# The second product of the last 30 token blocks, made of seven half products instead of eight

## The chip, the cores and the metric

The kernel runs on one core of one Trainium2 chip. The metric is the device time of one execution in microseconds (us), the median of several runs. The core's engines work side by side and wait for each other through semaphores: PE (TensorE, matmuls; its weight loads are shown as PEld), DVE (VectorE), ACT (ScalarE), POOL (GpSimd) and SP (SyncE, which here issues DMAs). ACT and POOL issue DMAs as well.

## The reference, cut to what matters

Two parts follow each other. The first filters a batch of 8 sequences of 2496 positions and 256 channels in the frequency domain; the second sends each of the 19968 positions (tokens) through one of 8 experts, chosen by a hash of its token id:

```
Y = np.fft.rfft(x, axis=1) * (filt_r + 1j * filt_i)
y = np.fft.irfft(Y, n=2496, axis=1)                 # then (8*2496, 256)
expert_idx = token_ids * np.int64(2654435761) % 8
for e in range(8):
    xe = y[expert_idx == e]
    h = np.maximum(xe @ w1[e], 0.0)                  # 256 -> 1024
    out[expert_idx == e] = h @ w2[e]                 # 1024 -> 256
```

All data is float32.

## The kernel before, in words

**The filter.** Each of the 8 batches (class Batch) goes through stages of matmuls with tables: stage1 (L225) to a DRAM buffer, forward (L269) with a product by the filter on DVE (L275 to L280), back (L292) to a second DRAM buffer, stage3 (L225 again). scatter (L382) writes the rows, by an indirect DMA of POOL, into a DRAM array xs that is sorted by expert into blocks of 256 tokens. Table d_t serves forward, e_t serves back, f_t holds the filters.

**The experts.** There are 80 sure blocks (NSURE) and 5 that are run only if there are tokens left. step(i) (L864) does one block. up(i) (L795) makes h = relu(x w1): both matrices are cut in halves, and the product is made by a scheme of Winograd's kind from 7 half products instead of 8, from sums of tokens (token_sums, L783, on DVE) and sums of weights (weight_sums, L792, on POOL, 4 per block). Its half products go to PSUM banks a, b and c; ACT copies one out (L813), DVE adds (L809) and ACT takes the relu (L806). down(i) (L832) makes h w2 in the plain way, 16 matmuls of 256 columns into bank d (L837), and DVE copies the result out (L842). store(i) (L844) writes the rows of a block, two indirect DMAs of POOL (L847). A float32 matmul stands in the trace as two passes.

**Loads.** load(i + 2) (L753, ACT queue, L762) brings the tokens of a block, token_parts (L773) transposes them on DVE. weights(i + 2, 0) and (i + 2, 1) (L395) issue on SP the loads of w1 (L413) and w2 (L416), 1 MB each, under a condition: only where the expert of the block is another than that of the block two earlier. Even and odd blocks have buffers of their own.

**The order.** It is written out by hand. In step(i) the queues get: on POOL weight_sums(i + 1), then store(i - 1); on PE up(i), then down(i); on DVE the sums of up(i), then token_parts(i + 1) and token_sums(i + 1), then the copy of down(i). The filter's pieces hang in a list of due times counted in blocks (todo), and run_until puts those that are due between the parts of a block: run_until(i + .6) after up, three more among the matmuls of down, one at the block's end. The filter's last pieces are due at block 47, so from block 48 on a block holds nothing else. The last stage of blocks, 50 to 79, holds the tokens of the last two batches and what was left of the others; its blocks go through the experts in ascending order, even blocks through one half of them and odd ones through the other.

The order of up's half products, with what reads each, is short enough to show:

```
product("a", w1[:, 0, 0:h], x[0, 0], True)
nc.scalar.copy(out=h21, in_=ps["a"][:])
product("b", t[1], st[:, 1, :], True)
plus(h12, "b", h21)
product("c", t[0], st[:, 0, :], True)
plus(h22, "c", h21)
```

Of the kernel before, what the change touches and what calls it, by code (L numbers as in the profile page):

```python
# [11 lines left out]
F32 = mybir.dt.float32  # L12
I32 = mybir.dt.int32
AF = mybir.ActivationFunctionType
OP = mybir.AluOpType
# [4 lines left out]
P = 128  # L20
# [26 lines left out]
DP = C // P  # L47
# [3 lines left out]
NPAD = NT * TB - N  # L51
NQP = NPAD // P
NSURE = NT - 5

# [64 lines left out]
def kernel(  # L119
# [16 lines left out]

    xs = nc.dram_tensor("xs", (NT * TB, W), F32)
    slot_dram = nc.dram_tensor("slots", (N,), I32)

    def pool(stack, name, bufs, space=None):  # L140
        kw = {} if space is None else {"space": space}
# [32 lines left out]
    def slot(kind):  # L174
        slots[kind].append(slots[kind].pop(0))
        return slots[kind][-1]

    put_off = []

# [215 lines left out]
    def weights(i, which):  # L395

        if i >= NT:
            return
        if i >= 2 and which == 0:
            ws[i] = ws[i - 2][0:2]  # L400
        eng, kw = nc.scalar if i < 2 else nc.sync, {}
        if which == 0:
            ws[i].append(eng.value_load(chunk_i[0:1, 0, i:i + 1], min_val=0, max_val=E - 1))
            if i >= 2:
                ws[i].append(eng.value_load(chunk_i[0:1, 1, i:i + 1], min_val=0, max_val=1))
        e = ws[i][2]
        if i >= 2:
            kw = {"cond": ws[i][3]}
        if which == 0:


            for f in (slice(0, F // 2), slice(F // 2, F)) if i < 2 else (slice(0, F),):
                eng.dma_start(out=ws[i][0][:, :, f],  # L413
                              in_=moe_w1[bass.ds(e, 1)].rearrange("one (p dp) f -> p (one dp) f", p=P)[:, :, f], **kw)
        else:
            eng.dma_start(out=ws[i][1], in_=moe_w2[bass.ds(e, 1)].rearrange("one (fp p) d -> p (one fp) d", p=P), **kw)  # L416


    rctx = ctx.enter_context(ExitStack())
# [357 lines left out]
    def token_sums(i):  # L777
        x = parts[i]
        st = work.tile([P, 4, P], F32, name=f"st_{i}", tag="st")
        for k, (p, q, op) in enumerate((((1, 0), (1, 1), OP.add), (0, (0, 0), OP.subtract),  # L780
                                        ((0, 0), (1, 0), OP.subtract), ((0, 1), 1, OP.subtract))):
# [62 lines left out]
    def store(i):  # L844
        o = rows.pop(i)
        for h in range(2):
# [13 lines left out]
    def run_until(t):  # L860
        while main and main[0][0] < t:
            main.pop(0)[1]()

    def step(i):  # L864
        ht = work.tile([P, 2, FP, P], F32, name=f"ht_{i}", tag="ht")
# [12 lines left out]
        run_until(i + 1)  # L878
# [56 lines left out]
```

## Time and profile before

| | |
|---|---|
| median of 3 runs | 1490.96 us (1489.63 to 1495.55) |
| the profiled execution | 1492.68 us, its span 1490.90 us |
| mean granted TensorE clock | 0.977 |
| block 50 begins, block 79 ends (PE) | 1083.2, 1478.0 us |
| matmuls of the second product, L837 | 589.5 us busy, 2560 passes, mean 384 ns |
| weight sums on POOL, L792 | 316 of 774 us of POOL, mean about 1.3 us each |
| DMA | 245.70 MB, 165 GB/s in the mean |

The span is the time from the first to the last recorded instruction; the execution's time has 1.8 us around it. A row of the timeline gives the start (us from the span's start), the time taken, the engine, the line, the operation with what it writes and reads, the shape, how many of them the row merges, and in brackets how long the engine had been idle before and what ended that. Ends of matmuls are modelled, so the pace of PE is read from start to start. A line in the chain or the groups is that of the kernel's file as printed above.

### The profile page before, as it was taken

The page shows a single profiled execution, that of the slowest core. Times are in us where ns is not written, and L with a number is a line of the kernel's source. Part 1 is how long each engine was busy: PE and PEld are TensorE (multiplying, and loading weights), DVE is VectorE, ACT ScalarE, POOL GpSimd, SP SyncE. Part 2 cuts the span into 40 slices and gives each one's busy share as a digit, 9 for nine tenths or more (in the row PEclk, how much of TensorE's full clock was granted, in tenths as well). Part 3 has the DMA queues.
Part 4 walks back from the last instruction along what each step waited for, and adds up shares of the span by engine and source line. Part 5 has one row for each costly group of instructions (what it writes and reads, how often), then busy time and mean ns, then how long its engine had stood idle before and what let it go on. Part 6 is the DMA issues. An engine that isn't in the chain of part 4 may idle for free.

```text
span 1490.9 us, 24354 instructions
## 1 busy us (share of the span) xinstructions
PE 1403.1 (94%) x8746; PEld 1278.3 (86%) x8746; DVE 826.6 (55%) x1374; ACT 401.4 (27%) x710; POOL 774.3 (52%) x700
## 2 busy tenths in 40 slices
PE   5996699999999979999989999999999999999996
PEld 5985688888888868888978999998999999999996
DVE  6772565475556547544655466543555555656463
ACT  2563122222233212322222222222222222222221
POOL 5056332763475455567533566577564545464551
PEclk8998799999999989999999999999999999999998
DMA  8248567747988596888834763556523324241412
GB/s 213 48 137 256 146 198 185 228 152 245 275 235 259 163 272 217 254 268 265 255 115 120 197 192 100 158 148 206 156 72 97 97 63 124 71 127 44 147 35 54
DMA packets 234104, 245.70 MB, mean 165 GB/s; under 512 B 128604, under 2 KB 206351, under 8 KB 226861
## 3 DMA queue, kind: packets, MB, share of 16 engines
q1 hardware_dynamic: 77079, 140.92, 31.0%
q10 hardware_dynamic: 136982, 58.59, 16.0%
q0 software_dynamic: 19920, 44.59, 8.7%
q8 instruction: 72, 1.18, 0.3%
q14 instruction: 51, 0.42, 0.1%
HBM read 251.19 MB, written 75.14 MB: 219 GB/s over the span
## 4 chain that ended last, share of the span: by engine, by line
PE 63%; DMA 4%; ACTq 1%; DVE 0%; ACT 0%; issue 0%; DVEq 0%; SPq 0%
PE dps L837 30%; PE up_b L802 11%; PE up_a L802 7%; PE up_c L802 7%; PE pd L225 3%; PE pc L292 2%; DMA t<-d 2%; PE pb L269 2%; DMA xg<-xs 1%; ACTq L762 1%; PE pa L225 1%; ACT ht L806 0%; DMA out_dram<-osb,no 0%; PE pd L219 0%; DMA wts<-in_moe_w_dram 0%
## 5 line engine op out<-in xcount | busy, mean ns | idle before, releaser
L837 PE MATMUL dps<-wts,ht 128*128 128x256 f32 x2560 | 589.5, 384 | 24.9 <-ACT ht L806 24.9
L837 PEld LDWEIGHTS dps<-wts,ht 128*128 128x128 f32 x2560 | 487.2, 192 | 96.8 <-ACT ht L806 29.3
L792 POOL TENSOR_TENSOR tw<-wts 128x512 f32<-128x512 f32 x158 | 204.6, 1295 | 214.1 <-DMA wts<-in_moe_w_dram 164.2
L382 POOL DMA_INDIRECT xs<-o,sidx x176 | 176.2, 1001 | 194.3 <-ACT o L227 83.7
L809 DVE TENSOR_TENSOR ht<-up_b,ht 128x512 f32<-128x512 f32 x240 | 166.0, 691 | 175.9 <-PE up_b L802 165.1
L847 POOL DMA_INDIRECT out_dram<-osb,no x160 | 158.9, 993 | 198.5 <-DVE osb L842 165.6
L806 ACT ACTIVATE ht<-ht 128x512 f32<-128x512 f32 x240 | 148.9, 629 | 339.5 <-DMA xg<-xs 151.5
L792 POOL TENSOR_TENSOR tw<-wts,tw 128x512 f32<-128x512 f32 x158 | 206.1, 1304 | 6.2
L802 PE MATMUL up_a<-xt,wts 128*128 128x128 f32 x1280 | 183.4, 276 | 16.3 <-DVE xt L773 16.3
L842 DVE COPY osb<-dps 128x512 f32<-128x512 f32 x80 | 55.4, 692 | 257.6 <-PE dps L837 257.5
L802 PEld LDWEIGHTS up_a<-xt,wts 128*128 128x128 f32 x1280 | 169.0, 193 | 21.6 <-POOL tw L792 16.7
L802 PE MATMUL up_b<-st,tw 128*128 128x128 f32 x1280 | 170.6, 276 | 2.8 <-DVE ht L809 1.2
L802 PEld LDWEIGHTS up_b<-st,tw 128*128 128x128 f32 x1280 | 156.6, 193 | 4.2 <-issue 2.8
L813 ACT COPY ht<-up_a 128x512 f32<-128x512 f32 x80 | 46.9, 586 | 370.5 <-PE up_a L802 344.1
L809 DVE TENSOR_TENSOR ht<-up_c,ht 128x512 f32<-128x512 f32 x160 | 110.6, 691 | 62.1 <-PE up_c L802 52.6
L279 DVE TENSOR_TENSOR z<-pb,filt 64x512 f32<-64x512 f32 x160 | 110.1, 688 | 36.4 <-PE pc L292 34.5
L783 DVE TENSOR_TENSOR st<-xt 128x128 f32<-128x128 f32 x160 | 103.8, 649 | 2.8
L275 DVE TENSOR_TENSOR y<-pb,filt 128x512 f32<-128x512 f32 x80 | 55.1, 689 | 68.8 <-PE pb L269 66.9
L802 PE MATMUL up_c<-st,tw 128*128 128x128 f32 x640 | 85.2, 276 | 0.0
L802 PE MATMUL up_b<-xt,tw 128*128 128x128 f32 x640 | 84.5, 275 | 0.0
L802 PE MATMUL up_c<-st,wts 128*128 128x128 f32 x640 | 84.5, 275 | 0.0
L802 PEld LDWEIGHTS up_c<-st,tw 128*128 128x128 f32 x640 | 78.6, 194 | 0.0
(142 smaller groups left out, 1324.3 us busy)
## 6 DMA issues: line engine op xcount, KB each, us to landing
wts<-in_moe_w_dram SPq DMA_DIRECT2D x160, 1024.0 KB
xg<-xs ACTq DMA_DIRECT2D x332, 64.0 KB
mid<-d SPq DMA_DIRECT2D x60, 256.0 KB
d<-mid ACTq DMA_DIRECT2D x60, 256.0 KB
d<-mid ACTq DMA_DIRECT2D x12, 960.0 KB
t<-d SPq DMA_DIRECT2D x12, 960.0 KB
x<-in_x_dram SPq DMA_DIRECT2D x36, 312.0 KB
x<-in_x_dram SPq DMA_DIRECT2D x21, 234.0 KB
```

The source lines that it names most:

```text
L225: nc.tensor.matmul(out=ps[0:cols * H, k, :], lhsT=w[:], rhs=src[:, 2 * i + k, :], start=True, stop=True)
L275: nc.vector.tensor_tensor(out=y[:], in0=ps[:], in1=f_t[0][:, sl, :], op=OP.mult)
L279: nc.vector.tensor_tensor(out=z[b], in0=ps[a], in1=f_t[1][64 * hi:64 * hi + 64, s1:s1 + 2, :], op=OP.mult)
L382: st = nc.gpsimd.indirect_dma_start(out=xs[:], out_offset=bass.IndirectOffsetOnAxis(ap=index, axis=0), in_=rows, in_offset=None, bounds_ch ...
L783: nc.vector.tensor_tensor(st[:, k, :], p, q, op=op)
L792: eng.tensor_tensor(t[k][:], p, q, op=OP.subtract)
L802: nc.tensor.matmul(out=ps[bank][:, f, :], lhsT=w[:, f * P:(f + 1) * P], rhs=xx, start=first and f == 0, stop=True, skip_group_check=True)
L806: nc.scalar.activation(out=out, in_=in_, func=AF.Relu)
L809: nc.vector.tensor_tensor(out, ps[bank][:], other, op=OP.add)
L837: nc.tensor.matmul(out=ps[:, h, :], lhsT=ht[:, h, fp, :], rhs=w2[:, fp, :], start=(fp == 0), stop=(fp == FP - 1))
L842: nc.vector.tensor_copy(out=rows[i][:], in_=ps[:])
L847: st = nc.gpsimd.indirect_dma_start(out=out[:], out_offset=bass.IndirectOffsetOnAxis(ap=to_rows[i][:, h:h + 1], axis=0), in_=o[:, h, :], i ...
```

## The change

From block 50 (WS = 50) a step goes to late_step(i), and that to both(i, ht), which makes both products. The second product is now also of Winograd's kind: h is cut in halves by tokens and by hidden columns, w2 in halves by rows and by columns, and the product comes from 7 half products of 4 matmuls of 128 columns each.

- **Sums of w2.** prepare(e, part) makes them once per expert: a load of w2[e] on SP, four sums on POOL (128x512 each) and a store of 1 MB on SP to the DRAM array t2_dram. The pieces are due from block 34.3 on, 1.5 blocks per expert, the last one at 47.1, among the filter's pieces. weights(i, 1) then loads 1 MB from t2_dram, behind w2 and under the same condition, for blocks 50 to 79, into the room of the tables d_t and e_t.
- **Sums of h.** Four sums of 128x512 on DVE, s[0] to s[3], in the room of the filter f_t[0].
- **Banks.** The first product takes two further PSUM banks (g and e, from the pool that the filter used), so that its 7 half products no longer wait for a bank that was just read; the second product takes banks b, d and two of that pool.
- **Order.** token_parts(i + 1) goes to the start of the block. Two token sums come between s[3] and the sums that read the second product, two after these. On POOL, the four weight sums now stand between the two stores of the block before: store half 1, weight_sums(i + 1), store half 0. w1's load is issued after the whole first product, as the last half product now reads w1.
- **Output.** Instead of one copy of 512 columns per block: two copies of 128 on ACT and six sums of 128 on DVE.

```diff
+    def prepare(e, part):
+        to = mid[:, 5 + 2 * (e % 2):7 + 2 * (e % 2), :].rearrange("p a b -> p (a b)")
+        if part == 0:
+            raw[e] = xpool.tile([P, FP, C], F32, name=f"raw_{e}", tag="x")
+            nc.sync.dma_start(out=raw[e][:], in_=moe_w2[e].rearrange("(fp p) c -> p fp c", p=P))
+        elif part < 5:
...
+            minus(nc.gpsimd, t[k], (b12, b22, b22, b21)[k], (b11, t[0], b12, t[1])[k])
+        else:
+            nc.sync.dma_start(out=t2_dram[e], in_=to)
...
             eng.dma_start(out=ws[i][1], in_=moe_w2[bass.ds(e, 1)]...)
+            if WS <= i < NSURE:
+                eng.dma_start(out=late["t2"][i % 2].rearrange("p k f c -> p (k f c)"),
+                              in_=t2_dram[bass.ds(e, 1)]..., **(kw if i >= WS + 2 else {}))
...
+    for e in range(E):
+        t = 34.3 + 1.5 * e
+        todo += within([(t + d, lambda e=e, k=k: prepare(e, k)) for k, d in enumerate((0, 1.1, 1.4, 1.7, 2, 2.3))])
...
+    def both(i, ht):
...
+        if i + 1 < NSURE:
+            token_parts(i + 1, late["xt"][i % 2])
+        product(a, w1[:, 0, 0:half], x[0, 0], True)
+        nc.scalar.copy(out=h21, in_=a[:])
+        if i + 2 < NT:
+            load(i + 2)
+        product(b, t[1], st[:, 1, :], True)
+        plus(h12, b[:], h21)
+        product(g, t[2], st[:, 2, :], True)
+        plus(h21, g[:], h12)
+        product(c, t[0], st[:, 0, :], True)
+        plus(h22, c[:], h21)
+        relu(h22, h22)
+        product(e, t[3], x[1, 1], True)
+        plus(h21, e[:], h21)
+        relu(h21, h21)
+        product(a, w1[:, 1, 0:half], x[0, 1], False)
+        relu(h11, a[:])
+        minus(nc.vector, s[:, 0], h21, h22, OP.add)
+        product(c, w1[:, 1, half:], st[:, 3, :], False)
+        plus(h12, c[:], h12)
+        relu(h12, h12)
+        weights(i + 2, 0)
...
+        second(e, h22, t2[:, 3], True)
+        second(c, s[:, 0], t2[:, 0], True)
+        second(a, h11, b11, True)
+        nc.scalar.copy(out=one, in_=a[:, 0, :])
+        minus(nc.vector, s[:, 1], s[:, 0], h11)
+        minus(nc.vector, s[:, 2], h11, h21)
+        minus(nc.vector, s[:, 3], h12, s[:, 1])
+        second(b, s[:, 1], t2[:, 1], True)
+        if i + 1 < NSURE:
+            token_sums(i + 1, late["st"][i % 2], range(2))
+        plus(o22, c[:, 0, :], one)
+        plus(o21, e[:, 0, :], one)
+        plus(o12, b[:, 0, :], one)
+        second(a, h12, b21, False)
+        nc.scalar.copy(out=o11, in_=a[:, 0, :])
+        if i + 1 < NSURE:
+            token_sums(i + 1, None, range(2, 4))
+        second(b, s[:, 2], t2[:, 2], False)
+        plus(o22, b[:, 0, :], o22)
+        plus(o21, b[:, 0, :], o21)
+        second(c, s[:, 3], b22, False)
+        plus(o12, c[:, 0, :], o12)
+        weights(i + 2, 1)
...
+    def late_step(i):
+        ht = work.tile([P, 2, FP, P], F32, name=f"ht_{i}", tag="ht")
+        store(i - 1, (1,))
+        if i + 1 < NSURE:
+            weight_sums(i + 1)
+        store(i - 1, (0,))
+        both(i, ht)
```

product and relu are as in up; plus(out, ps, other) is a sum on DVE with one input from PSUM, minus a sum or difference of two SBUF inputs, and second(ps, a, b, first) is four matmuls of 128 columns that add into the same 128 columns of ps:

```
for f in range(4):
    nc.tensor.matmul(out=ps[:, 0, :], lhsT=a[:, f, :], rhs=b[:, f, :],
                     start=first and f == 0, stop=True, skip_group_check=True)
```

More of the change, by code (lines that the diff above doesn't have):

```diff
@@ L53 @@
 NSURE = NT - 5
+WS = 50
 def stage_tiles():
@@ L138 @@
     slot_dram = nc.dram_tensor("slots", (N,), I32)
+    t2_dram = nc.dram_tensor("t2s", (E, P, FP * C), F32)
     def pool(stack, name, bufs, space=None):
@@ L176, in slot, with minus @@
         return slots[kind][-1]
+    spare = f_t[0][:].rearrange("p s c -> p (s c)")
+    late = {"t2": [t[:].rearrange("p s c -> p (s c)")[:, 0:FP * C].rearrange("p (k f c) -> p k f c", k=4, c=P)
+                   for t in (d_t, e_t)],
+            "sums": spare[:, 0:FP * C].rearrange("p (k f c) -> p k f c", k=4, c=P),
+            "xt": [spare[:, FP * C + 512 * k:FP * C + 512 * k + 512].rearrange("p (d h t) -> p d h t", d=DP, h=2)
+                   for k in range(2)],
+            "st": [spare[:, FP * C + 512 * k:FP * C + 512 * k + 512].rearrange("p (k t) -> p k t", k=4)
+                   for k in range(2, 4)],
+            "one": spare[:, FP * C + 2048:FP * C + 2048 + P]}
+    def minus(eng, out_, a, b, op=OP.subtract):
+        eng.tensor_tensor(out_, a, b, op=op)
+    raw = {}
+    def prepare(e, part):
[4 more added lines that the diff above has]
+        elif part < 5:
+            b11, b12, b21, b22 = [raw[e][:, 4 * f:4 * f + 4, P * c:P * c + P] for f in range(2) for c in range(2)]
+            t = [to.rearrange("p (k f c) -> p k f c", k=4, c=P)[:, k] for k in range(4)]
+            k = part - 1
+            minus(nc.gpsimd, t[k], (b12, b22, b22, b21)[k], (b11, t[0], b12, t[1])[k])
+        else:
+            nc.sync.dma_start(out=t2_dram[e], in_=to)
     put_off = []
@@ L416, in weights @@
             eng.dma_start(out=ws[i][1], in_=moe_w2[bass.ds(e, 1)].rearrange("one (fp p) d -> p (one fp) d", p=P), **kw)
+            if WS <= i < NSURE:
+                eng.dma_start(out=late["t2"][i % 2].rearrange("p k f c -> p (k f c)"),
+                              in_=t2_dram[bass.ds(e, 1)].rearrange("one p k -> p (one k)"), **(kw if i >= WS + 2 else {}))
     rctx = ctx.enter_context(ExitStack())
@@ L775, in token_parts, with token_sums @@
         parts[i] = {(h, d): xt[:, d, h, :] for h in range(2) for d in range(DP)}
-    def token_sums(i):
+    def token_sums(i, to=None, which=range(4)):
         x = parts[i]
-        st = work.tile([P, 4, P], F32, name=f"st_{i}", tag="st")
-        for k, (p, q, op) in enumerate((((1, 0), (1, 1), OP.add), (0, (0, 0), OP.subtract),
-                                        ((0, 0), (1, 0), OP.subtract), ((0, 1), 1, OP.subtract))):
+        st = parts[i].get("sums", to)
+        if st is None:
+            st = work.tile([P, 4, P], F32, name=f"st_{i}", tag="st")
+        for k in which:
+            p, q, op = (((1, 0), (1, 1), OP.add), (0, (0, 0), OP.subtract),
+                        ((0, 0), (1, 0), OP.subtract), ((0, 1), 1, OP.subtract))[k]
             p, q = [st[:, v, :] if isinstance(v, int) else x[v] for v in (p, q)]
@@ L842, in down, with bank, product, second @@
         nc.vector.tensor_copy(out=rows[i][:], in_=ps[:])
-    def store(i):
-        o = rows.pop(i)
-        for h in range(2):
+    def both(i, ht):
+        w1, w2 = ws[i][0:2]
+        x, st, t = parts[i], parts[i]["sums"], sums[i]
+        t2, s, one = late["t2"][i % 2], late["sums"], late["one"]
+        h11, h12, h21, h22 = [ht[:, h, 4 * f:4 * f + 4, :] for h in range(2) for f in range(2)]
+        b11, b12, b21, b22 = [w2[:, 4 * f:4 * f + 4, P * c:P * c + P] for f in range(2) for c in range(2)]
+        half = F // 2
+        def bank(k, name):
+            p, tag = (banks[k], k) if k in banks else (fps, "f")
+            return p.tile([P, 4, P], F32, name=f"{name}_{i}", tag=tag)
+        def product(ps, w, xx, first):
+            for f in range(4):
+                nc.tensor.matmul(out=ps[:, f, :], lhsT=w[:, f * P:(f + 1) * P], rhs=xx,
+                                 start=first and f == 0, stop=True, skip_group_check=True)
+        def second(ps, a, b, first):
+            for f in range(4):
+                nc.tensor.matmul(out=ps[:, 0, :], lhsT=a[:, f, :], rhs=b[:, f, :],
+                                 start=first and f == 0, stop=True, skip_group_check=True)
+        def relu(out, in_):
+            nc.scalar.activation(out=out, in_=in_, func=AF.Relu)
+        def plus(out, ps, other):
+            nc.vector.tensor_tensor(out, ps, other, op=OP.add)
+        a, b, c = [bank(k, "up" + k) for k in "abc"]
+        g, e = bank("f", "upg"), bank("f", "upe")
+        if i + 1 < NSURE:
[21 more added lines that the diff above has]
+        weights(i + 2, 0)
+        e, a = bank("b", "dne"), bank("d", "dna")
+        b, c = bank("f", "dnb"), bank("f", "dnc")
+        rows[i] = outs.tile([P, 2, C], F32, name=f"osb_{i}", tag="osb")
+        o11, o12, o21, o22 = [rows[i][:, h, P * k:P * k + P] for h in range(2) for k in range(2)]
+        second(e, h22, t2[:, 3], True)
[21 more added lines that the diff above has]
+        weights(i + 2, 1)
@@ L847, in store @@
+    def store(i, halves=range(2)):
+        o = rows[i]
+        for h in halves:
             st = nc.gpsimd.indirect_dma_start(
@@ L862, in run_until @@
             main.pop(0)[1]()
+    def late_step(i):
[5 more added lines that the diff above has]
+        both(i, ht)
     def step(i):
+        if i >= WS:
+            late_step(i)
+            return
         ht = work.tile([P, 2, FP, P], F32, name=f"ht_{i}", tag="ht")
```

## The prediction

> **What bounds the kernel now.** I read the page's first part, then the table of stretches, then the timeline of one block late in the run.
>
> ```profile
> PE 1403.1 (94%) x8746; PEld 1278.3 (86%) x8746; DVE 826.6 (55%) x1374; ACT 401.4 (27%) x710; POOL 774.3 (52%) x700
> ```
>
> TensorE is busy for 94% of the span; the two stretches this change touches say more (PE, PEld, DVE, ACT, POOL busy us, granted clock, DMA share, GB/s):
>
> ```profile
> 836.00:1044.00 208.00, 208.00 (x1314) 190.85 (x1314) 109.30 (x196) 55.67 (x99) 136.41 (x122) 1.00 0.57 164
> 1083.20:1478.00 394.80, 394.80 (x2641) 369.81 (x2639) 222.59 (x325) 88.90 (x150) 203.85 (x175) 1.00 0.31 85
> ```
>
> The first holds blocks 34 to 46, where the new sums are made; the second holds blocks 50 to 79, where they are used. In both PE never rests and its clock is full. A block's copy of the result (L842) comes every 13.16 us from block 46 to 79 (1201.82, 1214.98, 1228.14), so blocks 50 to 79 are 30 x 13.16 = 394.8 us. What a block costs is what PE's passes cost:
>
> ```profile
> 1201.62 1.05 PE L802 MATMUL up_a<-xt,wts 128*128 128x128 f32 x8
> ...
> 1207.87 7.07 PE L837 MATMUL dps<-wts,ht 128*128 128x256 f32 x32
> ...
> 1214.78 1.05 PE L802 MATMUL up_a<-xt,wts 128*128 128x128 f32 x8
> ```
>
> From start to start the first product takes 6.25 us for 56 recorded passes of 128 columns (111.6 ns each, 0.893 us per half product of 8 passes), the second 6.91 us for 32 passes of 256 columns (216 ns each). The weight load before each pass is hidden in both.
>
> **What is removed and added on PE.** In blocks 50 to 79 the 32 passes of 256 columns give way to 7 half products x 8 = 56 passes of 128 columns. These have the form of the passes of the first product, weight load and 128 moving columns included, so 56 x 111.6 ns = 6.25 us: 0.66 us less per block, 30 x 0.66 = **19.8 us** if nothing makes PE wait.
>
> The Trainium skill ("TensorE: Matmul & The Clock Gate", Back-to-back issue gap) speaks against it: in a stream of weight loads and matmuls it gives about 81 ns at 128 columns and 131 ns at 512, by my straight line 98 ns at 256, so that halving the columns saves only 17%. By that rule 56 passes of 0.83 x 216 ns would take 10.0 us, 3.1 us more per block and 94 us in all. The up passes above, each with its own weight load, have the rule's form and halve almost fully; I go by them.
>
> **The new waits.** Each block adds on DVE four sums of 512 columns (s0 to s3), and six small sums from PSUM in place of one copy of 512; PE now waits for DVE in the middle of the second product. I set the block's timetable, t = 0 where PE starts up_a, product k ending at 0.893 k. Delays come from these rows:
>
> ```profile
> 493.02 0.59 ACT L813 COPY ht<-up_a 128x512 f32<-128x512 f32 x1 [1.19 <-PE up_b L802]
> ...
> 493.64 0.69 DVE L809 TENSOR_TENSOR ht<-up_b,ht 128x512 f32<-128x512 f32 x1 [2.56 <-ACT ht L813]
> ...
> 494.25 0.68 DVE L809 TENSOR_TENSOR ht<-up_c,ht 128x512 f32<-128x512 f32 x1
> ...
> 494.48 0.79 PE L802 MATMUL up_b<-st,tw 128*128 128x128 f32 x5
> ```
>
> ACT's end to DVE 0.03; DVE to the next independent DVE operation of 512 columns 0.61; DVE's end to PE 0.15. From the block at 1201.62: PE to DVE 0.20, DVE to ACT 0.04, DVE to POOL 0.28.
> - h21 is summed from product e (ends 4.47): DVE 4.67 to 5.36, relu on ACT (0.63) 5.40 to 6.03, so s0 may start at 6.06 and end at 6.75. PE wants s0 at 7.14 (2nd half product): 0.24 to spare.
> - DVE then runs without rest: h12 6.69, s1 7.32, s2 7.93, s3 8.56, two token sums 9.17 and 9.50 (128x128 rows: 0.33 to a dependent one, 0.21 to the next), then o22 9.76, o21 9.97, o12 10.18 to 10.47. Only then may PE add into that bank again: 10.62, and PE gets there at 10.71. **0.09 us to spare**: the tight place.
> - The small sums read PSUM; the trace has no such row of 128x128. Below: 0.20 us (the 128x40 copy from PSUM, L524). Above: 0.69 as for 512 columns; three at 0.61 steps would end 1.2 us later, PE would wait 1.1 us, and each block would lose 0.45. I take 0.29, the 128x128 sum from SBUF, with the 1x128 copy from PSUM (L649, 0.28) beside it.
>
> Queued behind the late o12 on DVE are two token sums, the two sums that end o21 and o22 and so POOL's store; none is due before the next block.
>
> **The lock between DVE and POOL.** A DVE sum with both inputs in SBUF beside a POOL sum waits for it; beside a POOL indirect DMA it doesn't:
>
> ```profile
> 880.85 0.99 POOL L382 DMA_INDIRECT xs<-o,sidx  x1 [0.30 <-issue]
> 880.97 0.69 DVE L280 TENSOR_TENSOR y<-y,z 128x512 f32<-128x512 f32 x1
> ...
> 883.23 1.27 POOL L792 TENSOR_TENSOR tw<-wts,tw 128x512 f32<-128x512 f32 x1
> ...
> 883.89 1.15 DVE L280 TENSOR_TENSOR y<-y,z 128x512 f32<-128x512 f32 x1
> ```
>
> The last ends 0.54 us after POOL's. s0 to s3 are such sums. The change puts POOL's four weight sums between the two stores of a block. The first store may start when o21 of the block before is done: 11.61 + 0.20 + 0.21 + 0.29 + 0.28 = 12.59, 0.09 in the new block. How POOL goes on (POOL alone, 960 to 1000 us):
>
> ```profile
> 970.47 0.99 POOL L382 DMA_INDIRECT xs<-o,sidx  x1 [0.30 <-issue]
> 971.48 1.30 POOL L792 TENSOR_TENSOR tw<-wts 128x512 f32<-128x512 f32 x1
> ...
> 975.33 1.27 POOL L792 TENSOR_TENSOR tw<-wts,tw 128x512 f32<-128x512 f32 x1
> ...
> 981.45 1.00 POOL L382 DMA_INDIRECT xs<-o,sidx  x1 [2.38 <-ACT o L227]
> ```
>
> 1.01 for the store and 5.12 for four sums: 1.10 to 6.22. s0, ready at 6.06, then ends at 6.22 + 0.54 = 6.76, as without a lock. I cost the lock at nothing; its cover is those 0.15 us. One POOL sum more in the window costs DVE some 0.63 (8.64 for 8.01 at the end of s1) and PE 0.54.
>
> For both tight places I put 0.05 us per block: **+1.5 us** (0 to 6, that is 0.2 per block).
>
> **Loads.** A change of expert brings the 1 MB of the new sums behind w2, on SP. In the block at 1214.78, w1 is issued at 1220.43 and POOL starts on it at 1225.46: 5.03 us. Changes come in pairs of neighbouring blocks (POOL starts its sums late at 1146.50 and 1159.88, 1225.46 and 1238.81, and so on: 4 pairs). Then w2 and sums go out at 12.7 and land after 10 us, the neighbour's w1 goes out at 18.9 and lands between 23.9 and 27.7, where POOL wants it at 26.1: 0 to 1.6 us late, by the lock about as much for PE. **+1.2 us** (0 to 6). The sums themselves are wanted at 31.3: in time.
>
> **The preparation** (blocks 34 to 46): 32 POOL sums of 128x512 at 1.28 = 41 us, 8 loads and 8 stores of 1 MB on SP. POOL is busy 136 of 208 us; PE doesn't wait for it now. In blocks 41 to 46 the rows above repeat every 14.89 us with 2.38 us idle; 2.67 more sums per block (4 per 1.5 blocks) take 3.4, so POOL falls behind by 1.0 a block, 6 us in all. The weight sums that PE needs next end at 976.60 and are due near 985.6: 9 us of cover. Without it the 6 us are PE's. The DMAs add 16.8 MB, 81 GB/s to 164; the page's slices go up to 275. SP's stores wait for POOL, and behind them queue weights a block ahead and tables 2.2 blocks ahead. **+1.5 us** (0 to 6).
>
> **Tail**: a 128-column sum in place of the 0.69 copy ends the last block: 0.2 less, both ends small.
>
> **Sum**: -19.8 + 1.5 + 1.2 + 1.5 - 0.2 = -15.8. The profiled execution took 1492.68 us (span 1490.90), 1.7 above the median of the three runs, 1490.96, within their spread; off the median, **1475 us**.
>
> **Rivals.**
> 1. *DVE's chain is longer than I have it*: PE waits 0.3 to 0.6 us in each block for o12. For: 0.09 us of slack rests on durations no row shows. Against: spaced rows of like size. 9 to 18 us back: 1480 to 1490.
> 2. *The lock, slower than before*: POOL's weight sums come 2 us or more later than worked out and two of them stand between s0 and s3. Each costs 0.63: 1.26 - 0.09 = 1.17 us of wait against 0.66 gained, +0.5 x 30 = 15, with the other terms 1509. It decides from the second POOL sum in that window; one (0.54) leaves a small gain. For: nothing but POOL's queue keeps them out. Against: the rows put their end at 6.2.
> 3. *POOL is the bound in blocks 41 to 46*: the preparation costs PE 6 us and the loads 6 more: 1484 at worst, 1481 as I take it.
>
> **Chances.** Forecast (1470 to 1480) 0.69; rival 1 0.13, rival 2 0.12, rival 3 0.06. The best case is 1490.96 - 20.0, with the spread of runs 1469. The range goes from 1469 to 1487, leaving out rival 2 and the end of rival 1. Faster by over 0.5% (about what a measurement of this kernel can tell from no change; below 1483.5): the forecast, a third of rival 1 and half of rival 3, 0.69 + 0.04 + 0.03 = 0.76; slower is rival 2, 0.12; the rest, 0.12, is within 0.5%.
>
> **What would show it.** Blocks 50 to 79 at 12.5 to 12.6 us; PE without idle at the second product's 2nd and 6th half products (s0, o12); s0 near 0.7 us and POOL's fourth weight sum ending before it; 128x128 sums from PSUM near 0.29; PE still full from 836 to 1044. Idle PE before the 6th half product with unslowed sums is rival 1; s1 to s3 above 1 us is rival 2. If a 128-column pass that adds into one region costs more than 111.6 ns, the main term is wrong.

## The result and the profile after

The changed kernel takes **1474.47 us** (median of 8 runs, 1471.17 to 1482.86); beside it the kernel before took 1491.18 us (8 runs, 1484.21 to 1495.55). The ratio is 0.9901 (95% interval 0.9876 to 0.9925). 1475 was forecast. The profiled execution took 1478.73 us, its span 1477.0, and its mean granted clock 0.977 as before. It lies 4.3 us above its own median; the account below is therefore made from trace to trace.

The page's first part of the changed kernel:

```profile
PE 1386.2 (94%) x9466; PEld 1285.2 (87%) x9466; DVE 890.2 (60%) x1644; ACT 417.0 (28%) x770; POOL 822.2 (56%) x732
```

PE has more instructions than before and is busy for 16.9 us less; DVE has taken 64 us. The two stretches, the second one ending where block 79 now ends (span, PE, PEld, DVE, ACT and POOL busy, granted clock, DMA share, GB/s):

```profile
836.00:1044.00 208.00, 207.47 (x1309) 190.08 (x1309) 128.72 (x193) 55.44 (x99) 166.81 (x146) 1.00 0.76 231
1083.20:1464.00 380.80, 379.57 (x3376) 378.23 (x3374) 265.09 (x597) 104.94 (x210) 213.17 (x176) 1.00 0.38 115
```

PE is still nearly full in both: it rests 0.5 us in the first and 1.2 us in the second. One block of the second stretch, from the timeline of the changed kernel:

```profile
1200.38 1.06 PE L899 MATMUL upa<-filt,wts 128*128 128x128 f32 x8
...
1205.29 1.26 POOL L832 TENSOR_TENSOR tw<-wts,tw 128x512 f32<-128x512 f32 x1
...
1206.43 0.69 DVE L191 TENSOR_TENSOR filt<-ht 128x512 f32<-128x512 f32 x1 [0.69 <-ACT ht L908]
1206.63 1.06 PE L904 MATMUL dne<-e_t,ht 128*128 128x128 f32 x8
1206.71 1.28 POOL L970 DMA_INDIRECT out_dram<-osb,no  x1 [0.16 <-issue]
...
1207.53 1.06 PE L904 MATMUL dnc<-e_t,filt 128*128 128x128 f32 x8
...
1210.41 0.29 DVE L911 TENSOR_TENSOR osb<-dnb,filt 128x128 f32<-128x128 f32 x1
...
1211.10 1.06 PE L904 MATMUL dnb<-e_t,filt 128*128 128x128 f32 x8
...
1212.89 1.06 PE L899 MATMUL upa<-filt,wts 128*128 128x128 f32 x8
```

From up_a to up_a the block takes 12.51 us instead of 13.16. The second product runs from 1206.63 to 1212.89: 56 passes in 6.26 us, 111.8 ns each. POOL's fourth weight sum ends 6.17 us after the block's start, before s0 (L191, 6.05 to 6.74) is half done, and s0 takes 0.69 us, unslowed. The last small sum before the return to bank b (o12, L911 reading dnb) ends at 10.32, and PE gets there at 10.72 without waiting.

Of PE's waits in blocks 50 to 79, a table of the trace (engine, what waits, for what: us in total, times, longest) names these:

```profile
PEld dnc L904 <- DVE filt L191: 1.5, 3, 0.8
PE dnc L904 <- DVE filt L191: 0.9, 3, 0.6
PEld upc L899 <- DVE ht L911: 0.2, 1, 0.2
```

That is three waits for s0, and a short one in the first product of block 56. The three belong to blocks 50, 56 and 68, which take 13.33, 13.22 and 12.95 us; block 66 takes 12.58, and all others 12.50 or 12.51.

Set beside the kernel before, block by block (the starts of up_a):

| stretch | before | after | difference |
|---|---|---|---|
| to block 34 | 835.70 | 837.77 | +2.07 |
| 34 to 50 (preparation) | 247.48 | 248.51 | +1.03 |
| 50 to 79 | 381.64 | 364.75 | -16.89 |
| block 79 | 13.16 | 12.50 | -0.66 |
| from the last pass to the end | 12.92 | 13.47 | +0.55 |
| span | 1490.90 | 1477.00 | -13.9 |

The first row compares the same instructions: the change has put nothing there. Without it the change is worth 16.0 us in the trace, beside 16.7 between the medians and 15.8 by the forecast's sum.

### The profile page after: what moved, and what is told of

It is laid out like the page before. It is cut to its first block, busy times and chain, and to the rows that moved or that the text cites. A ratio compares the mean times of both kernels' runs of the same rounds, so it can differ in the third digit from the quotient of the medians.

```text
span 1477.0 us, 26433 instructions
## 1 busy us (share of the span) xinstructions
PE 1386.2 (94%) x9466; PEld 1285.2 (87%) x9466; DVE 890.2 (60%) x1644; ACT 417.0 (28%) x770; POOL 822.2 (56%) x732
## 3 DMA queue, kind: packets, MB, share of 16 engines
q8 instruction: 77, 1.26, 0.3%
## 4 chain that ended last, share of the span: by engine, by line
PE 59%; DMA 8%; DVE 1%; ACTq 1%; ACT 1%; issue 1%; SPq 0%; DVEq 0%
PE dps L877 16%; PE up_b L842 5%; PE dnc L904 4%; PE dna L904 4%; PE dnb L904 4%; DMA t<-d 3%; PE upa L899 3%; PE upc L899 3%; PE up_a L842 3%; DMA xg<-xs 3%; PE up_c L842 3%; PE pd L256 2%; PE pc L323 2%; PE pb L300 2%; PE upe L899 2%; PE upg L899 2%
## 5 line engine op out<-in xcount | busy, mean ns | idle before, releaser
L877 PE MATMUL dps<-wts,ht 128*128 128x256 f32 x1600 | 378.5, 388 | 27.6 <-ACT ht L846 27.6
L877 PEld LDWEIGHTS dps<-wts,ht 128*128 128x128 f32 x1600 | 307.2, 194 | 76.9 <-ACT ht L846 32.5
L832 POOL TENSOR_TENSOR tw<-wts 128x512 f32<-128x512 f32 x158 | 203.7, 1290 | 109.6 <-DMA wts<-in_moe_w_dram 79.4
L832 POOL TENSOR_TENSOR tw<-wts,tw 128x512 f32<-128x512 f32 x158 | 205.8, 1302 | 6.2
L849 DVE TENSOR_TENSOR ht<-up_b,ht 128x512 f32<-128x512 f32 x150 | 103.7, 691 | 112.0 <-PE up_b L842 102.3
L842 PE MATMUL up_a<-xt,wts 128*128 128x128 f32 x800 | 115.6, 278 | 16.1 <-DVE xt L810 16.1
L882 DVE COPY osb<-dps 128x512 f32<-128x512 f32 x50 | 34.6, 692 | 155.0 <-PE dps L877 154.4
L842 PEld LDWEIGHTS up_a<-xt,wts 128*128 128x128 f32 x800 | 106.3, 194 | 19.6 <-POOL tw L832 16.5
L842 PE MATMUL up_b<-st,tw 128*128 128x128 f32 x800 | 107.6, 278 | 3.1 <-DVE ht L849 1.4
L842 PEld LDWEIGHTS up_b<-st,tw 128*128 128x128 f32 x800 | 98.5, 194 | 4.6 <-issue 2.5
L256 PE MATMUL pd<-t,wi_t 120*117 120x256 f32 x320 | 76.1, 380 | 1.3 <-DVE t L386 1.3
L311 DVE TENSOR_TENSOR y<-y,z 128x512 f32<-128x512 f32 x80 | 72.5, 907 | 2.7
L258 ACT COPY o<-pd 117x512 f32<-117x512 f32 x80 | 45.5, 586 | 99.3 <-PE pd L256 76.6
```

The source lines that it names most:

```text
L256: nc.tensor.matmul(out=ps[0:cols * H, k, :], lhsT=w[:], rhs=src[:, 2 * i + k, :], start=True, stop=True)
L311: nc.vector.tensor_tensor(out=y[:], in0=y[:], in1=z[:], op=OP.add)
L832: eng.tensor_tensor(t[k][:], p, q, op=OP.subtract)
L842: nc.tensor.matmul(out=ps[bank][:, f, :], lhsT=w[:, f * P:(f + 1) * P], rhs=xx, start=first and f == 0, stop=True, skip_group_check=True)
L849: nc.vector.tensor_tensor(out, ps[bank][:], other, op=OP.add)
L877: nc.tensor.matmul(out=ps[:, h, :], lhsT=ht[:, h, fp, :], rhs=w2[:, fp, :], start=(fp == 0), stop=(fp == FP - 1))
```

## The experiments

Eleven kernels were run. "Blocks" is the usual length of a block in the last stretch, "50 to 79" the time between the starts of these two. Each ratio is against the kernel before on the same chip; the first seven ran on two chips where that took 1491.55 and 1492.05 us, the last four on a third where it took 1508.61 us.

| kernel | ratio (95%) | blocks | 34 to 50 | 50 to 79 |
|---|---|---|---|---|
| before | 1 | 13.16 | 247.48 | 381.64 |
| the change | 0.9901 (0.9876 to 0.9925) | 12.50 | 248.51 | 364.75 |
| e1_stores_first | 0.9973 (0.9951 to 0.9995) | 12.75 | 249.11 | 375.38 |
| e2_sums_first | 1.0613 (1.0573 to 1.0653) | 12.5 to 18.7 | 249.6 | 470.5 |
| e3_tokens_early | 0.9937 (0.9901 to 0.9974) | 12.62 | 249.46 | 369.18 |
| e4_prepare_only | 1.0018 (0.9998 to 1.0039) | 13.16 | 249.08 | 381.64 |
| e5_t2_later | 0.9907 (0.9877 to 0.9937) | 12.50 | 249.63 | 363.51 |
| e6_tail | 0.9925 (0.9896 to 0.9955) | 12.50 | 247.93 | 363.52 |
| e7_narrow_plain | 1.0043 (1.0013 to 1.0072) | 13.40 | 247.47 | 388.60 |
| e8_prepare_dma | one run | 13.16 | 248.09 | 381.64 |
| e9_prepare_sums | one run | 13.16 | 250.14 | 381.64 |
| e10_sums_early_at_50 | 0.9869 (0.9835 to 0.9902) | 12.50 | 250.62 | 362.69 |
| e11_layout | 0.9920 (0.9889 to 0.9950) | 12.50 | 250.17 | 363.52 |

The theory after the result was that of the forecast: the gain is the pace of narrow passes, it survives because two tight places on DVE hold, and the rest is lost to the preparation, to loads at a change of expert and at the tail. The rivals: POOL's place on the queue doesn't matter, a narrow pass into one region is slower than an up pass and something else gave the time, or the stalls of blocks 50, 56 and 68 have another cause than the loads and the first store.

### e1 and e2: the order on POOL

e1_stores_first puts both stores ahead of the weight sums, so that these end one store later:

```diff
-        store(i - 1, (1,))
+        store(i - 1, (1, 0))
         if i + 1 < NSURE:
             weight_sums(i + 1)
-        store(i - 1, (0,))
```

> Both stores of the block before go ahead of the four weight sums on POOL, so the sums run 1.3 us later. Theory of the lock: the fourth sum then stands between s0 and s1; s1 waits for it and ends 0.65 us later, PE's wait before the sixth half product of the second product is 0.65 less the 0.25 us that the changed kernel's trace leaves there: 0.4 us a block, the block 12.9 us instead of 12.51, the kernel about 12 us above the changed one, near 1486. Rival (the order on POOL doesn't matter, since DVE and POOL share without waiting): blocks stay at 12.51 us and the time near 1474.

Measured: ratio 0.9973, blocks 12.75 and 12.76 but for blocks 50, 53, 54 and 56. The timeline of this kernel, POOL and DVE of one block:

```profile
1207.72 0.75 DVE L191 TENSOR_TENSOR filt<-ht 128x512 f32<-128x512 f32 x1 [0.70 <-ACT ht L908]
1207.87 1.73 POOL L832 TENSOR_TENSOR tw<-wts,tw 128x512 f32<-128x512 f32 x1
...
1208.99 1.16 DVE L191 TENSOR_TENSOR filt<-filt,ht 128x512 f32<-128x512 f32 x1
```

The fourth weight sum (L832) now lies between s0 and s1. It takes 1.73 us instead of 1.26, as it waits for s0, and s1 takes 1.16 instead of 0.68, as it waits for the weight sum. The 0.48 us run down DVE's chain, and PE waits for o12. The waits of e1, from block 50 on:

```profile
PEld dnb L904 <- DVE osb L911: 6.8, 26, 2.3
```

One of these waits, in block 53, is 2.3 us long; the other 25 are about 0.18 us each, and by its length a block loses 0.25 us to 12.50, less than the 0.4 expected: 0.48 less a slack of 0.23. Blocks 53 and 54 take 15.67 and 13.47. In block 53 POOL's second store starts 2.68 us late, for a reason that the trace doesn't name, and three of the four weight sums fall among s0 to s3. PE in this block:

```profile
1133.67 1.21 PE L904 MATMUL dnb<-e_t,filt 128*128 128x128 f32 x8 [2.08 <-DVE osb L911]
1134.68 1.92 PE L904 MATMUL dnc<-wts,filt 128*128 128x128 f32 x8
```

One store's place on a queue costs seven tenths of the gain by the ratios; of the 10.6 us that the stretch is longer in this trace than in the change's, 4.1 are these two blocks.

e2_sums_first goes the other way, the weight sums of the next block ahead of both stores:

```diff
-        store(i - 1, (1,))
         if i + 1 < NSURE:
             weight_sums(i + 1)
-        store(i - 1, (0,))
+        store(i - 1, (1, 0))
```

> The four weight sums go ahead of both stores, as in the kernel before; they then start when the next load of w1 is issued, 6.5 us into a block, and all four stand among s0 to s3 and the token sums. Theory of the lock: DVE and POOL take turns, each of s1, s2, s3 and the first token sum waits 0.6 to 1.3 us, PE waits 3 to 4.5 us a block, blocks of 15.5 to 17 us, the kernel at 1565 to 1605 us, slower than the one before. Rival (no lock, or a small one): blocks of 12.5 to 13 us, 1474 to 1490.

Measured: ratio 1.0613, 1582.49 us; 17 of the 30 blocks take 17.4 to 18.7 us, more than was expected, and the others 12.5 to 16.5. The timeline of e2:

```profile
1206.52 1.27 POOL L832 TENSOR_TENSOR tw<-wts 128x512 f32<-128x512 f32 x1 [3.78 <-DMA wts<-in_moe_w_dram]
...
1207.05 1.29 DVE L191 TENSOR_TENSOR filt<-filt,ht 128x512 f32<-128x512 f32 x1
...
1208.26 1.75 DVE L191 TENSOR_TENSOR filt<-ht 128x512 f32<-128x512 f32 x1
...
1209.94 1.75 DVE L191 TENSOR_TENSOR filt<-ht,filt 128x512 f32<-128x512 f32 x1
...
1211.11 1.71 POOL L832 TENSOR_TENSOR tw<-wts,tw 128x512 f32<-128x512 f32 x1
...
1213.94 2.05 PE L904 MATMUL dnb<-e_t,filt 128*128 128x128 f32 x8 [3.27 <-DVE osb L911]
```

With no store ahead of the sums, POOL comes to them a block earlier: after the stores of block i - 1 it is at once at the sums of block i + 2. These wait for weights(i + 2, 0), which SP reaches only after the first product (the 3.78 us, put down to w1's DMA). So the four sums start beside s1, and the two engines take turns through s1 to s3. PE waits 3.27 us for o12. Where the expert changes, w1's transfer holds the sums back until s3 is done, and the block keeps its 12.5 us. That wait costs more than itself: the eight passes after it take 2.05 us instead of 1.06. The stretches of e2 before it, right after it, and of the end of the next block, where a wait of 3.30 us ends at 1231.64, show it in the column before the last two, the granted clock:

```profile
1206.00:1213.00 7.00, 4.67 (x42) 4.47 (x41) 6.97 (x7) 1.46 (x4) 6.22 (x4) 1.00 0.00 0
1213.00:1219.00 6.00, 5.06 (x30) 5.06 (x31) 2.69 (x10) 0.45 (x1) 1.25 (x2) 0.72 0.06 23
1231.00:1236.00 5.00, 4.36 (x27) 4.36 (x28) 2.38 (x9) 0.04 (x1) 0.99 (x1) 0.66 0.00 0
```

What follows: the lock between the two engines is real in this kernel, and which side of s0 to s3 POOL's sums fall on decides between a gain of 1% and a loss of 6%. That was the slower rival of the forecast, with four sums in the window instead of two.

### e3: the slack at o12, measured

e3_tokens_early puts all four token sums ahead of the three small sums, where the change has two:

```diff
-            token_sums(i + 1, late["st"][i % 2], range(2))
+            token_sums(i + 1, late["st"][i % 2], range(4))
...
-        if i + 1 < NSURE:
-            token_sums(i + 1, None, range(2, 4))
```

> All four token sums stand ahead of the sums that empty the second product's banks, instead of two. Theory of the tight DVE chain: 0.42 us more ahead of o12. By the prediction's slack of 0.09 us PE waits 0.33 us a block (blocks of 12.83 us, 1484 us); by the slack that the changed kernel's trace shows, 0.25 us, it waits 0.17 us (blocks of 12.68 us, 1480 us). Rival (the chain isn't tight): 12.51 us and 1474.

Measured: blocks 12.62 and 12.63. The timeline of e3:

```profile
1210.65 1.01 DVE L823 TENSOR_TENSOR filt<-filt 128x128 f32<-128x128 f32 x4
...
1211.99 0.28 DVE L911 TENSOR_TENSOR osb<-dnb,filt 128x128 f32<-128x128 f32 x1
1212.32 1.16 PE L904 MATMUL dnb<-e_t,filt 128*128 128x128 f32 x8
```

In this block, which begins at 1201.59, o12 ends at 10.68 instead of 10.32, for the two sums put in DVE's way; PE's next half product after the one into bank b begins 0.12 us later than in the change. So 0.36 us of delay cost 0.12: the slack there is about 0.25 us and not the 0.09 of the forecast.

### e4, e8 and e9: what the preparation costs

e4_prepare_only takes the way to late_step out of step: the sums are made and stored, and loaded but not used.

```diff
     def step(i):
-        if i >= WS:
-            late_step(i)
-            return
```

> The sums of w2 are made, stored and loaded as in the changed kernel, but every block is done in the plain way, so nothing uses them. Theory (the preparation lies beside PE's work and costs little): blocks 34 to 49 together 1 us longer than before, blocks 50 to 79 at 13.16 us, 1491 to 1493 us. Rival (POOL's backlog or the added loads reach PE): 3 to 6 us more in blocks 34 to 49, 1494 to 1498 us.

Measured: ratio 1.0018, blocks 34 to 50 249.08 us, 1.6 longer than before. Over the change and e1 to e6, which hold the whole preparation, this stretch takes 247.93 to 249.63, in the mean 1.6 more than before. Two things make up nearly all of it in e4: block 37 takes 19.47 instead of 19.21, and block 47 14.45 instead of 13.16. Issue and second product of block 47 in the timeline of e4:

```profile
1044.20 3.50 ACTq L799 DMA_DIRECT2D xg<-xs  x4
...
1049.41 7.17 PE L877 MATMUL dps<-wts,ht 128*128 128x256 f32 x32 [1.03 <-ACT ht L846]
```

ACT issues the token loads of block 49 in 3.50 us, where it takes 1.82 in the kernel before, and begins 1 us later; the relu stands behind them on the same queue, and PE waits 1.03 us for it. e1, e2, e3 and e5 lose 1.3 to 1.9 us in block 47; the issue takes 3.21 to 3.56 us there and begins 1.2 to 1.6 us late. In the change and in e6 it takes 2.67 and 2.90 and begins in time, which is hidden. So it depends on the execution whether block 47 pays.

What the issue waits for is named by the chain of waits of e5:

```profile
1033.73 1.32 POOL mid L191
...
1035.07 0.36 SPq L207
...
1035.77 1.83 SPq L447
...
1039.58 8.57 DMA wts<-in_moe_w_dram
...
1048.18 0.31 ACTq L803
...
1049.05 1.12 ACT ht L850 x2
```

A preparation sum on POOL ends late. SP's store of the sums (L207) waits for it, and the loads of w2 (L447) and w1 stand behind this store on SP. In the kernel before, w1's load goes out 5.65 us into block 46, in the change and e1 to e6 at 11.0 to 11.9. It lands after 8.57 us, and only then does ACT's last token load go out (L803), with the relu behind it. The chains of e2 and e3 have the same steps. Why the issue of a token load waits for w1 to land isn't shown.

e8_prepare_dma keeps the transfers alone (part 5 stores the raw rows, the sums are left out), e9_prepare_sums the POOL sums alone (from the table d_t in place of a loaded w2, with a store of 64 bytes per partition). Both leave the later loads and late_step out.

```diff
# e8
         elif part < 5:
+            return
...
-            nc.sync.dma_start(out=t2_dram[e], in_=to)
+            nc.sync.dma_start(out=t2_dram[e], in_=raw[e][:].rearrange("p f c -> p (f c)"))
# e9
-            raw[e] = xpool.tile([P, FP, C], F32, name=f"raw_{e}", tag="x")
-            nc.sync.dma_start(out=raw[e][:], in_=moe_w2[e].rearrange("(fp p) c -> p fp c", p=P))
+            raw[e] = d_t[:].rearrange("p s c -> p (s c)")[:, 0:FP * C].rearrange("p (f c) -> p f c", c=C)
...
-            nc.sync.dma_start(out=t2_dram[e], in_=to)
+            nc.sync.dma_start(out=t2_dram[e][:, 0:16], in_=to[:, 0:16])
```

> Only the transfers of the preparation: w2 is loaded and stored per expert (1 MB each way, at the same places on SP), POOL makes no sums, nothing is loaded from the store later, all blocks plain. It leaves out the sums of w2. Looked at: blocks 34 to 49, 247.47 to 247.48 us without a preparation, 249.1 with it. Theory of the transfers (a token load that ACT issues waits for a transfer of 1 MB issued before it, ACT's relu comes late, PE waits): 248.3 to 249.6 us. Rival (POOL's backlog is what reaches PE): 247.5.

> Only the sums of the preparation: POOL makes its 32 sums from a table that lies in SBUF, no load, a store of 8 KB in place of 1 MB, all blocks plain. It leaves out the load of w2. Blocks 34 to 49: theory of the transfers 247.5 to 247.8 us; rival, POOL's backlog: about 249.

Measured: e8 248.09 (+0.6), e9 250.14 (+2.7). I had expected the transfers to carry the cost; in these two runs, one of each, the sums carry more of it. On the same chip the whole preparation costs 3.1 us (e10, 250.62) and 2.7 (e11, 250.17). Block 37 takes 19.44 in e9 and 19.20 in e8, so its 0.24 are the sums'. Blocks 42 to 46 of e9 take 0.2 to 0.75 us longer each. Two rows of its table of waits:

```profile
PE up_b L838 <- DVE ht L845: 0.8, 2, 0.4
...
PEld up_b L838 <- POOL mid L191: 0.6, 1, 0.6
```

L191 writing mid is the preparation's sum, but PE doesn't wait for POOL here. The weight sums of that block, 46, had ended at 1043.94, over 10 us before; PE's row of the same half product waits for a DVE sum that ends 0.15 us ahead of it. This sum started 0.92 us later behind its own half product than the same one in block 47, with DVE idle. Such waits stand in blocks 43 and 44 of e8, 43 to 45 of e10 and 43 to 46 of e11 too, all on this chip; what holds DVE isn't shown.

Block 47, where most of the cost lies in e4, is 13.16 in e8 and e9: w1's load goes out 5.66 and 5.65 us into block 46, and ACT's issue takes 1.82 us in e8 and 2.42 in e9. The long issue was seen only with the transfers and the sums together. In the change itself it came in another block, 42, which takes 15.66 instead of 14.89; the timeline of the changed kernel:

```profile
977.87 0.63 ACT L846 ACTIVATE ht<-ht 128x512 f32<-128x512 f32 x1 [4.03 <-DMA t<-d]
```

Again the relu stands behind the issue of token loads, which ended at 977.82, and PE waits 0.51 us. The chain names a load of the filter (t, 960 KB) that SP issued right behind a store of sums (966.19 and 966.60) and that took 10.82 us to land. So the preparation costs 0.24 us in block 37 by POOL's sums and 0 to 1.9 us by ACT's issues, which wait for loads held back on SP; on the third chip, of which there is no trace without any preparation, it costs 2.7 to 3.1 us, most of it in waits of DVE whose cause is open.

### e5 and e10: the stalls of blocks 50, 56 and 68

e5_t2_later issues the load of the new sums for the next block after that of w1 for the block behind it, in place of right behind w2:

```diff
-            if WS <= i < NSURE:
-                eng.dma_start(out=late["t2"][i % 2]...)
+            if i == WS:
+                load_t2(i)
...
         weights(i + 2, 0)
+        if i + 1 < NSURE:
+            load_t2(i + 1)
```

> The load of the w2 sums of a block is issued half a block later, behind the load of the next block's w1 (the first one, of block 50, stays). Theory (where the expert changes, 2 MB at once keep back the token load and the next w1): the two waits of 0.71 and about 0.5 us in blocks 56 and 67 to 68 of the changed kernel go, the 0.82 us of block 50 stays; blocks 51 to 79 at 12.51 us throughout, about 1.2 us less in all, 1473. Rival (the waits come from the loads' mere number of bytes): they stay or move to other blocks.

Measured: all blocks of the stretch 12.50 or 12.51 but block 50, 13.33; the stretch 1.24 us shorter, which is what blocks 56, 66 and 68 had lost. The later kernels with this order, e6, e10 and e11, have none of these waits either. In the run's time (ratio 0.9907) it can't be seen. What the loads do is seen in the changed kernel, blocks 56 and 68:

```profile
1163.24 2.67 ACTq L799 DMA_DIRECT2D xg<-xs  x4
...
1164.77 0.71 DVE L810 STREAM_TRANSPOSE filt<-xg 128x512 f32<-128x512 f32 x1 [2.13 <-DMA xg<-xs]
...
1169.90 1.16 PE L904 MATMUL dnc<-d_t,filt 128*128 128x128 f32 x8 [0.15 <-DVE filt L191]
```

```profile
1314.80 1.27 POOL L832 TENSOR_TENSOR tw<-wts 128x512 f32<-128x512 f32 x1 [0.73 <-DMA wts<-in_moe_w_dram]
...
1319.07 1.38 DVE L191 TENSOR_TENSOR filt<-ht 128x512 f32<-128x512 f32 x1 [0.70 <-ACT ht L908]
```

In block 68 w1 lands 0.73 us late, POOL's sums shift into s0, and the block loses 0.45 us: the way the forecast had it. In block 56 it is the tokens that land late: DVE waits 2.13 us for them at the block's start and the whole chain to s0 moves.

From block 34 to block 79 nothing of the 1.24 us is left in the profiled execution of e5, for its block 47 takes 15.06 us (the issue on ACT's queue) where the change's took 13.16.

Block 50 stays at 13.33 in e5. In the changed kernel:

```profile
1087.44 0.97 POOL L970 DMA_INDIRECT out_dram<-osb,no  x1 [9.22 <-DVE osb L882]
...
1092.27 1.28 POOL L832 TENSOR_TENSOR tw<-wts,tw 128x512 f32<-128x512 f32 x1
1092.33 1.76 DVE L191 TENSOR_TENSOR filt<-ht 128x512 f32<-128x512 f32 x1 [0.70 <-ACT ht L908]
```

Block 49 is still of the old kind: its result is copied out whole (L882), the first store waits for that, the four weight sums run 1 us late, and s0 meets the fourth: 1.76 us. e10_sums_early_at_50 is e5 with the weight sums ahead of both stores in this one block, where w1 has long been there:

```diff
-        store(i - 1, (1,))
+        if i > WS:
+            store(i - 1, (1,))
         if i + 1 < NSURE:
             weight_sums(i + 1)
-        store(i - 1, (0,))
+        store(i - 1, (0,) if i > WS else (1, 0))
```

> The kernel with the later load of the w2 sums, and in block 50 alone POOL makes its weight sums ahead of both stores, as before; block 49 is plain, so its late copy no longer pushes them against s0. Theory of the lock: the 0.83 us that block 50 is longer than the others goes, all of blocks 50 to 78 at 12.51 us, 362.7 us from block 50's to block 79's start instead of 364.75; in time 2 us below the changed kernel, 1472 to 1474, which a measurement can hardly tell. Rival (block 50's wait is that of its first load): 13.3 us stays.

Measured: block 50 takes 12.50 too, and 50 to 79 is 362.69, nothing left over the pace of PE. Its ratio, 0.9869 (0.9835 to 0.9902), is the best of all, but its interval overlaps with the change's.

### e6 and e11: the end of the kernel

The chain of waits of the changed kernel ends in loads and transposes of the five spare blocks' tokens. Its last lines:

```profile
1472.01 1.97 DMA xg<-xs
...
1474.10 0.71 DVE mid L810
```

e6_tail is e5 with these loads on SP in blocks 70 to 74 and their transposes in blocks 72 to 76, so that behind block 79 only its stores are left:

```diff
-        if i + 2 < NT:
+        if i + 2 < NSURE:
             load(i + 2)
...
+        if NSURE - 10 <= i < NSURE - 5:
+            load(i + 10)
...
-    store(NSURE - 1)
+    store(NSURE - 1, (1, 0))
-    for i in range(NSURE, NT):
-        token_parts(i, ...)
```

> As the kernel with the later load, and the tokens of the five spare blocks are loaded (SP, blocks 70 to 74) and transposed (DVE, blocks 72 to 76) into the room of the filter f_t[1] instead of after the last block. Theory (after the last pass of PE, 13.4 us go by in a chain of loads and transposes of blocks that are not run): the end comes 5 to 7 us after the last pass, the time 7 us lower, near 1466; the added 0.7 us of DVE per block in five blocks fits into DVE's idle time at the block's start. Rival (the end is set by the last stores and what the program does after them): 1471 to 1473.

Measured: 1479.78 us, ratio 0.9925. The theory fell. The stretch 50 to 79 paid nothing for the moved work (363.52), but from PE's last pass to the end it is still 11.9 us, 1.6 less than in the change. The last store of e6, at 1466.56 of a span of 1477.1:

```profile
1466.56 0.97 POOL L987 DMA_INDIRECT out_dram<-osb,no  x1 [0.30 <-issue]
```

From its end to the span's end it takes 9.5 us; in the change, 9.9 us (1467.06 to 1477.0), before, 9.5 (1481.39 to 1490.9). The end hangs on the last store; the chain's last lines ran beside that. What fills this time stands in the view of L1064, the `with` statement under which the program's last instructions are recorded; the timeline and the chain leave such instructions of a queue out. In the changed kernel:

```profile
L1064 POOLq DRAIN  x3: 46/103/5132, 1471.1 to 1476.7; - x3
```

POOL's queue first waits until the last store has landed (2.05 us in the kernel before, 2.55 in the change, 2.10 in e6), then spends 1.43 us on an instruction INC_SWDGE_SEM and 5.13 us on this DRAIN; 0.8 us of semaphores follow. The 1.43 and 5.13 are the same in all traces. The 1.6 us of e6 are the store: it lands sooner, and it starts 1.2 us earlier, as e6 also swaps the last two stores and so puts first the half that is ready first.

What stands against the 1.6 us in e6's time are its first 34 blocks: 687.8 us in its profiled execution, against 677.7 to 683 in the other kernels of the first two chips. These blocks hold the same instructions in all. e6 has one small tile more in the pool keep, which shifts what lies behind it; e11_layout is e5 with such a tile and its clearing alone.

> The kernel with the later load, with one small tile more among the first ones, so that what lies behind it in SBUF moves by 40 bytes per partition; nothing else changes. If the kernel with the early spare loads was slow in its first 34 blocks because of where things lie: 1478 to 1481 us, and 686 to 689 us for these blocks in its trace. If that was chance: near 1475 and 678 to 683 us.

Measured: ratio 0.9920 (0.9889 to 0.9950), beside e5's 0.9907. This neither shows nor excludes an effect of the layout. What is seen is that these blocks differ by up to 10 us between the traces of the first chips, and take 689.0 to 700.5 us in the four of the third. That most of the spread of the run times comes from there is likely, but not shown.

### e7: the pace of narrow passes by itself

e7_narrow_plain is the kernel before, with the second product of blocks 50 to 79 still plain, eight half products, but in passes of 128 columns: 64 passes in place of 32.

```diff
+            for c in range(2 if 50 <= i < NSURE else 0):
+                for fp in range(FP):
+                    nc.tensor.matmul(out=ps[:, h, c * P:c * P + P], lhsT=ht[:, h, fp, :],
+                                     rhs=w2[:, fp, c * P:c * P + P], start=(fp == 0), stop=(fp == FP - 1))
```

> The kernel before, with the second product of blocks 50 to 79 in the plain way but by 128 columns: 64 passes instead of 32 of 256. It measures the pass alone. Theory (a pass costs by its columns, 111.6 ns): 7.14 us for 6.91, blocks of 13.39 us, 6.9 us more than before, 1498. Rival (the page's rule for streams of weight loads and matmuls, 0.83 of the 256-column pass): 11.5 us, blocks of 17.7 us, 1628.

Measured: blocks 13.40 us, ratio 1.0043. The chain of waits of e7 has the product as one step:

```profile
1476.25 7.16 PE dps L838 x64
```

7.16 us for 64 passes are 111.9 ns each, against 6.91 us for 32 of 256 columns. A pass of half the width costs 52% of the wide one, and of the 0.89 us that one half product less would save per block, the narrow form gives 0.24 back before anything waits.

## Why the prediction was right, step by step

| step | forecast | measured |
|---|---|---|
| PE's passes | -19.8 | -19.6 (30 blocks by 0.653) |
| both tight places | +1.5 | +0.8 (block 50; nothing in the others) |
| loads at a change of expert | +1.2 | +1.2 (blocks 56, 66, 68) |
| preparation | +1.5 | +1.0 in this trace, +1.6 over seven kernels, +2.7 and +3.1 on the third chip |
| tail | -0.2 | +0.55 |
| sum | -15.8 | -16.0 |

That the sum agrees within 0.2 us is luck: single terms are off by up to 0.75 us in both directions, and the runs of one kernel spread over more than 11 us. What carries the result is the first term.

- **The pace.** Taking 111.6 ns from the up passes was right: 111.8 in the change, 111.9 in e7. By the estimate that the forecast made from the Trainium skill ("TensorE: Matmul & The Clock Gate", Back-to-back issue gap), e7's product would have been 11.5 us long (64 passes of 0.83 x 216 ns). It took 7.16, and the measurement decides.
- **The tight places.** s0 was put at 6.06 to 6.75 and came at 6.05 to 6.74; POOL's end was put at 6.22 and came at 6.17. The second place was mis-sized: o12 was put at 10.47 with 0.09 us to spare and came at 10.32 with 0.25. Of the 0.15 us, 0.10 are there when s3 starts (8.46 instead of 8.56): the sums of 512 columns follow each other in 0.60 to 0.61 us, dependent ones too, for which 0.63 was taken. The rest is o22, which comes 0.20 us behind the token sum instead of 0.26; the small sums from PSUM take 0.28 or 0.29 us each, as taken. e3 gives the same slack by another way. The 0.05 per block were therefore nothing, and the 0.8 of block 50 came from a step that the forecast didn't look at: the first late block follows one whose result comes out later.
- **The loads.** The size fits, and e5 shows the cause. Only half of the mechanism was as told: w1 came late in block 68, but the tokens in block 56.
- **The preparation.** The size fits on the first chips, on the third it is half of what was measured. The mechanism fits in part. POOL's backlog was priced as one that PE meets in its weight sums; in the change POOL's sums cost 0.24 us (block 37). That SP's stores wait for POOL, with weights and tables behind them, was named but given no price, and this is where block 47 of e1 to e5 loses its time. The last step is missing in the forecast: ACT's issue of token loads waits until w1 has landed, and the relu stands behind it. The term came out right by luck, because it was put between nothing and 6 us and a small part of that was taken.
- **The tail** was mis-sized. It was costed by the last sum on DVE; what counts is when the last store is issued. That now ends 3.5 us after PE's last pass (1463.53 to 1467.06) instead of 3.4, and 9.9 us follow it instead of 9.5; of the 0.55 us most is the time until this store has landed.
- **The rivals.** Rival 1 is excluded by the waits: none is for o12. Rival 2 is real, but not in this order: e1 pays 0.25 per block and e2 5 to 6 in most. Its price for one POOL sum (0.63 on DVE, 0.54 on PE) was 0.48 and 0.25 in e1. For four sums a price per sum no longer tells the time, because of the clock. Rival 3, that PE waits for POOL in blocks 41 to 46, is shown in no run; its 6 us stand against 2.7 to 3.1 on the third chip, by waits of DVE.

## What to carry to other kernels

A saving of arithmetic is worth what the passes take at their new width, measured from rows of the same form, and it holds only as long as each sum that it adds is done before PE asks for it: write the timetable of one block with both engines and look for the smallest slack. Where two engines share a lock, one instruction's place on the other engine's queue can be worth more than the change, so look at each block where the order enters that state anew, the first one above all. And before work is moved out of an end that the chain of waits names, ask what else ends at the same moment, and look at the instructions of the queues that the chain leaves out.

## What the runs showed of the hardware

- **A wait of PE costs its clock too.** In e2 a wait of 3.27 us is followed by 6 us with a granted clock of 0.72, and one of 3.30 by 0.66; the eight passes after the first take 2.05 us in place of 1.06. The mean clock of the run is 0.95 instead of 0.977. In e1 a wait of 2.08 us is followed by the same (0.72 from 1132 to 1138 us, eight passes in 1.92 us), while one of 2.20 us in e2 that ends at 1197.89 leaves the clock at 1.00, as do the waits of 0.2 to 0.6 us in the change. The Trainium skill ("TensorE: Matmul & The Clock Gate", Part 1: The HAM clock gate) says that the clock is halved after at least one idle window of about 3.4 us. The waits of e2 lie just under that and the pace of the passes agrees, but the wait of e1 is well under it: the length of a wait alone doesn't decide here.
- **POOL and DVE lengthen each other**: a POOL sum 1.27 to 1.73 us, a DVE sum with two SBUF inputs 0.68 to between 1.16 and 1.76. A POOL indirect DMA beside such DVE sums takes 1.28 instead of 0.98, and the DVE sums stay at 0.68.
- **An issue of a DMA can hold an engine.** ACT's issue of four token loads takes 1.8 to 1.9 us in many blocks and up to 3.56 in others, and the compute behind it on the queue waits: PE waited 0.5 to 1.6 us each time that this came through. In e5 the issue waited until a load of w1, issued on SP, had landed after 8.57 us.
- **The end**: 9.5 to 9.9 us from the end of the last store's instruction to the end of the span, in three kernels: 2.05 to 2.55 us until the store has landed, then 1.43 and 5.13 us for two instructions of POOL's queue and 0.8 us of semaphores.
